# Cosine attention and a low-rank mixer on one core: transposing q and k by the DMA queue instead of TensorE from the ninth head pair on

## The chip, the core and the metric

The kernel runs on one core of a Trainium2 chip. A core has five engines that run side by side: TensorE (PE in the profile; its weight loads are PEld), VectorE (DVE), ScalarE (ACT), GpSimd (POOL) and SyncE (SP, which here only issues DMAs). Sixteen DMA engines move data between the main memory (DRAM), and SBUF, the memory on chip; a DMA can also go from SBUF to SBUF. TensorE writes its results to PSUM. The metric is the device time of one execution in microseconds (us). Before the change it is 648.73 us, the median of 9 runs (648.23 to 649.25).

## The reference

For 8 batches, 12 heads, 448 positions and 64 channels per head:

```python
q_n = q / (np.linalg.norm(q, axis=-1, keepdims=True) + 1e-06)
k_n = k / (np.linalg.norm(k, axis=-1, keepdims=True) + 1e-06)
scores = np.matmul(q_n, k_n.transpose(0, 1, 3, 2)) / tau
attn = softmax(scores)            # written out in the reference
x = (attn @ v) heads side by side # (8, 448, 768)
u = x + (x.transpose(0, 2, 1) @ U @ V).transpose(0, 2, 1)   # U 448x32, V 32x448
out = u + np.maximum(u @ w_ch1, 0) @ w_ch2                  # 768 -> 3072 -> 768
```

The scores need q and k with the 64 channels along the partitions, so both are transposed after they have been normalised.

## The kernel before

**Pairs and slots.** Two heads are worked on together. There are 48 pairs, 6 for each batch. The main loop (from L507) goes over 49 slots; slot n issues, in this order, the parts: `step_S` of pair n, first half; `step_V` of pair n-1, first half; `step_S`, second half; `step_V`, second half; `step_T` of pair n+1; `step_A` and `step_H` of pair n-1.

- `step_T` (L254) transposes the normalised q and k of a pair on TensorE: eight 128x128 transposes (L260) into the PSUM tile `tp`, one VectorE copy (L262) into the SBUF tile `qkT`, of which there are three in turn.
- `step_S` (L268) reads `qkT`: seven matmuls for the scores (L282, L274) and their exponentials on ScalarE (L284, L276).
- `step_V` (L290) multiplies with the values (L302, L309), and VectorE divides by the sums (L315, L316) into `X`.
- `step_A` and `step_H` (L327, L345) apply the low-rank mixer and add x; their result is u of the batch.

**Filling work.** Each batch's two large matrix products (`steps_m1`, L363, and `steps_m2`, L390 and L399) are cut into steps of about 1 us, put in a list when the batch's attention is finished, and handed out between the parts of the next batch's slots, in proportion to the parts' weights (`weights`, L520). The first such work is handed out in slot 7; what is left after the last slot runs at the end. ScalarE or VectorE takes each step's result out of PSUM, whichever a running estimate (`est`) finds free first.

**Loads and normalising.** q, k and v come in groups of mostly two pairs. Three sets of staging tiles (`qst`, `kst`, `vst`) are used in turn. A group's ten loads are issued on SP at the end of the slot before a group three earlier begins (L500, `load_all`). `Prep` normalises a group, m being its first pair: squares on GpSimd in slot m-3, sums, roots and reciprocals in slot m-2, and in the same slot the scaling (`scale`, L241), of k on GpSimd into `kb`, of q on VectorE into `qn`. The weight matrices are loaded on the GpSimd queue in slots 1 to 4.

**What sets the order.** Every engine's order is the order in which the program issues its instructions; nothing is rearranged. SP's queue holds, in that order, the loads of q, k and v and the stores of the output (L416, L419, L422), which wait until the `o_sb` tile is filled. An instruction that waits holds up all behind it on its engine. Eight semaphores are used in turn for SP's DMAs, so that each DMA waits for the eighth before it.

Of the kernel before, what the change touches and what calls it, by code (L numbers as in the profile page):

```python
# [10 lines left out]
BF = mybir.dt.bfloat16  # L11
# [11 lines left out]
def kernel(  # L23
# [16 lines left out]
    nc = tc.nc  # L40

    B, H, S, D = q.shape
# [3 lines left out]
    NP = H // 2  # L46
# [5 lines left out]
    const = ctx.enter_context(tc.tile_pool(name="const", bufs=1))  # L52
    work = ctx.enter_context(tc.tile_pool(name="work", bufs=2))
# [5 lines left out]
    class Estimate:  # L59


        def __init__(self):
            self.t = {"pe": 0.0, "act": 0.0, "dve": 0.0}
# [22 lines left out]

    NG = 4
    NST = 3
    qst, kst, vst, kbs, v65 = [], [], [], [], []
    for i in range(NST):  # L90
        for lst, nm in ((qst, "qst"), (kst, "kst"), (vst, "vst")):
            lst.append(const.tile([128, NG, 4, D], FP, name=f"{nm}{i}"))
        kbs.append(const.tile([128, NG // 2, 4, 2, D], BF, name=f"kb{i}"))
        v65.append(const.tile([128, NG, 4, D + 1], BF, name=f"v65_{i}"))
    for i in range(NST):
        nc.vector.memset(qst[i][64:128, :, 3, :], 0.0)
# [3 lines left out]
    ident = const.tile([128, 128], BF, name="ident")  # L100
# [7 lines left out]
    for i in range(2):  # L108
        t = const.tile([128, 7, 512], BF, name=f"E{i}")
# [75 lines left out]
    norm = {}  # L185

    class Prep:


        def __init__(self, gi):  # L190
            self.gi = gi
            _, _, self.n = groups[gi]
            self.nh = 2 * self.n
            self.s = gi % NST
            self.early = gi < 2
            self.ss = self.inv = self.qn = None
            self.sq = {}

        def flat(self, t):
# [34 lines left out]
            est.dve(0.55)  # L234

        def scale(self, i, j, eng):
            if self.qn is None:
                self.qn = work.tile([128, NG // 2, 4, 2, D], BF, name="qn", tag="qn", bufs=2)
            t, o = ((qst[self.s], self.qn), (kst[self.s], kbs[self.s]))[i]
            iv = self.inv[:, i, 8 * j:8 * j + 8].rearrange("p (h c) -> p c h", c=4)  # L240
            eng.tensor_mul(o[:, j, :, :, :],  # L241
                           t[:, 2 * j:2 * j + 2, :, :].rearrange("p h c d -> p c h d"),
                           iv.unsqueeze(3).to_broadcast([128, 4, 2, D]))
            if eng is nc.vector:
                est.dve(0.79)
            norm[self.gi] = (self.qn, kbs[self.s], v65[self.s])

        def values(self):
            nc.gpsimd.tensor_copy(out=self.flat(v65[self.s])[:, :, 0:D], in_=self.flat(vst[self.s]))
# [2 lines left out]
    qkT = {}  # L252

    def step_T(b, p):  # L254
        gi, j = group_of[(b, p)]
        qn, kb, _ = norm[gi]
        tp = psum.tile([128, 8, 128], BF, name="tp", tag="ps_x", bufs=1)
        for i, t in ((0, qn), (1, kb)):
            for c in range(4):
                nc.tensor.transpose(out=tp[:, 4 * i + c, :], in_=t[:, j, c, :, :], identity=ident)  # L260
        t = work.tile([128, 2, 512], BF, name="qkT", tag="qkT", bufs=3)
        nc.vector.tensor_copy(out=t.rearrange("p a b -> p (a b)"),  # L262
                              in_=tp.rearrange("p a b -> p (a b)"))
        qkT[(b, p)] = t
        est.pe(0.46)
        est.dve(0.69)

    def step_S(b, p, cs):  # L268
        t = qkT[(b, p)]
        e = E[(b * NP + p) % 2]  # L270
        for c in cs:
            sc = psum.tile([128, 2, 512], FP, name="sc", tag="ps_sc", bufs=2)
            if c == 3:
                nc.tensor.matmul(out=sc[:, 0, 0:S], lhsT=t[:, 1, 384:512], rhs=t[:, 0, 0:S],  # L274
                                 start=True, stop=True)
                nc.scalar.activation(out=e[:, 6, 0:S], in_=sc[:, 0, 0:S], func=AF.Exp)  # L276
                est.pe(0.3)
                est.act(0.56)
                continue
            for h in range(2):  # L280
                r = slice(64 * h, 64 * h + 64)
                nc.tensor.matmul(out=sc[:, h, 0:S], lhsT=t[r, 1, c * 128:(c + 1) * 128],  # L282
                                 rhs=t[r, 0, 0:S], start=True, stop=True)
            nc.scalar.activation(out=e[:, 2 * c:2 * c + 2, 0:S], in_=sc[:, :, 0:S], func=AF.Exp)  # L284
            est.pe(0.25)
            est.act(0.93)
# [2 lines left out]

    def step_V(b, p, half):  # L290
        gi, j = group_of[(b, p)]
        vv = norm[gi][2]
        e = E[(b * NP + p) % 2]
        if half == 0:
            X_of[(b, p)] = work.tile([128, 4, 128], BF, name="X", tag="X", bufs=2)
        X = X_of[(b, p)]
        bank = psum.tile([128, 512], FP, name="av", tag="ps_av", bufs=1)
        av_of[(b, p)] = bank
        av = bank[:, 0:4 * (D + 1)].rearrange("p (i h d) -> p i h d", i=2, h=2)
        for i in range(2):  # L300
            ic = 2 * half + i
            nc.tensor.matmul(out=av[:, i, :, :], lhsT=e[:, 6, ic * 128:(ic + 1) * 128],  # L302
                             rhs=vv[:, 2 * j:2 * j + 2, 3, :],
                             start=(i == 0), stop=False, skip_group_check=True)
        for i in range(2):
            ic = 2 * half + i
            for h in range(2):
                for c in range(3):
                    nc.tensor.matmul(out=av[:, i, h, :],  # L309
                                     lhsT=e[:, 2 * c + h, ic * 128:(ic + 1) * 128],  # L310
                                     rhs=vv[:, 2 * j + h, c, :],
                                     start=False, stop=(i == 1 and h == 1 and c == 2),
                                     skip_group_check=True)
        rd = work.tile([128, 4, 1], FP, name="rd", tag="rd", bufs=4)
        nc.vector.reciprocal(out=rd, in_=av.rearrange("p i h d -> p (i h) d")[:, :, D:D + 1])  # L315
        nc.vector.tensor_mul(  # L316
            X[:, 2 * half:2 * half + 2, :].rearrange("p i (h d) -> p i h d", h=2),
            av[:, :, :, 0:D],
            rd.rearrange("p (i h) o -> p i h o", h=2).to_broadcast([128, 2, 2, D]))
        est.pe(0.52)  # L320
        est.dve(0.6)
# [23 lines left out]
    def step_H(b, p):  # L345
        up = up_of[(b, p)]
        nc.tensor.matmul(out=up, lhsT=A_of[(b, p)], rhs=V_sb,  # L347
                         start=False, stop=True, skip_group_check=True)
        nc.vector.tensor_copy(out=u_of(b)[:, p, 0:S], in_=up)  # L349
        est.pe(0.19)  # L350
        est.dve(0.62)
        if b % 2 == 1 and p == NP - 1:
            nc.vector.tensor_copy(out=uO[:, :, S:512], in_=uE[:, :, 384:S])
# [77 lines left out]
    pairs = [(b, p) for b in range(B) for p in range(NP)]  # L431
# [36 lines left out]
    place_mixer()  # L468
    g1.reduce(1)
    step_T(*pairs[0])  # L470
    g1.reduce(0)
    g1.root()
# [9 lines left out]
    for gi in range(1, len(groups)):  # L482
        m, n, g = first_pair[gi], groups[gi][2], preps[gi]
# [23 lines left out]
    for n in range(NPAIR + 1):  # L507
        b, p = pairs[n] if n < NPAIR else (B, 0)
        prev = pairs[n - 1] if n > 0 else None
        now, nxt = n < NPAIR, n + 1 < NPAIR  # L510
        parts = [
            now and (lambda: step_S(b, p, (0, 1))),
            prev and (lambda: step_V(*prev, 0)),
            now and (lambda: step_S(b, p, (2, 3))),
            prev and (lambda: step_V(*prev, 1)),
            nxt and (lambda: step_T(*pairs[n + 1])),
            prev and (lambda: step_A(*prev)),
            prev and (lambda: step_H(*prev)),
        ]
        weights = [w if part else 0 for part, w in zip(parts, (2, 2, 2, 2, 2, 2, 1))]  # L520
        left = NP - p + 0.85 if p else 0.85
        nf = len(fill) if p == 0 else int(round(len(fill) / left))
        given = acc = 0
        for fn in after.pop((n, -1), []):
            fn()
        for i, (fn, w) in enumerate(zip(parts, weights)):
            if fn:
                fn()
            for g in after.pop((n, i), []):
                g()  # L530
            acc += w
            want = nf * acc // sum(weights)
            for _ in range(min(want - given, len(fill))):
                fill.pop(0)()
            given = want
        if p == 0 and n > 0:
            while fill:
                fill.pop(0)()
            fill.extend(steps_m1(b - 1) + steps_m2(b - 1))
# [38 lines left out]
```

## Time and profile before

| | |
|---|---|
| median of 9 runs | 648.73 us |
| the profiled execution: its own time, its span | 649.25 us, 647.5 us |
| TensorE busy | 609.6 us (94%) |
| VectorE, ScalarE, GpSimd busy | 273.3, 273.4, 195.1 us |
| L260, transposes on TensorE | 384, 219 ns each at the median |
| L262, VectorE's copy of a pair's transposes | 48, 687 ns in the mean |
| DMA traffic | 54.33 MB, mean 84 GB/s |

A line of the profile's groups names a source line, an engine, an operation, the tiles it writes and reads, its shapes and its count. Durations of TensorE's matmuls overlap one another, so that the time one takes up is read from the start of one to the start of the next in the timeline. In the timeline, a line is start, length, engine, line, operation, tiles, count, and in brackets idle time before it and what ended it. SPq is SP's queue: the time at which a DMA is issued, not the time that it takes. The table of DMA issues has the median time from issue to landing.

### The profile page before, as it was taken

What the parts mean: (1) busy time and instruction counts of PE and PEld (TensorE: products, weight loads), DVE (VectorE), ACT (ScalarE), POOL (GpSimd) and SP (SyncE); (2) the same over time, 40 slices, a digit from 0 to 9 for tenths busy, and PEclk for the clock granted to TensorE, in tenths of its full rate; (3) what the DMA queues carried; (4) which work ended last, traced back from release to release, by engine and by line L of the source; (5) the groups of instructions that cost most, each with busy time, mean ns of one, the idle gap of its engine ahead of it and who ended that gap; (6) DMA issues with size and microseconds to landing.
All of it is one profiled execution on the core that took longest, in us unless ns stands there. A gap on an engine that the chain in (4) does not pass through costs nothing.

```text
span 647.5 us, 12173 instructions
## 1 busy us (share of the span) xinstructions
PE 609.6 (94%) x5160; PEld 360.6 (56%) x5160; DVE 273.3 (42%) x524; ACT 273.4 (42%) x501; POOL 195.1 (30%) x158
## 2 busy tenths in 40 slices
PE   1467999999999999999999999999999999999997
PEld 0244556665566556665566655665566655665564
DVE  4688334355344454354352553463442543210000
ACT  2465554435433454344433455334523454424310
POOL 7877243042140341340431431431404401000000
PEclk9997999999999999999999999999999999999999
DMA  7799991350315420161315303044301100011012
GB/s 190 197 218 234 233 238 51 93 152 2 86 29 131 110 71 18 27 172 48 86 26 135 93 23 82 25 115 108 87 19 32 50 1 1 25 25 26 1 49 49
DMA packets 51782, 54.33 MB, mean 84 GB/s; under 512 B 5552, under 2 KB 48112, under 8 KB 51728
## 3 DMA queue, kind: packets, MB, share of 16 engines
q1 hardware_dynamic: 44288, 43.14, 25.9%
q0 software_dynamic: 7120, 10.18, 8.6%
q8 instruction: 40, 0.66, 0.4%
q10 hardware_dynamic: 320, 0.23, 0.1%
q14 instruction: 14, 0.11, 0.1%
HBM read 52.02 MB, written 11.01 MB: 97 GB/s over the span
## 4 chain that ended last, share of the span: by engine, by line
PE 91%; DVE 6%; DMA 2%; SPq 0%; issue 0%; ACT 0%; ACTq 0%
PE mp L390 34%; PE mp L363 34%; PE av L309 5%; PE sc L282 5%; PE tp L260 3%; PE sc L274 2%; DVE qn L241 2%; PE av L302 2%; PE av L331 2%; PE up L342 1%; PE mp L399 1%; DVE ss L215 1%; PE up L347 1%; DMA qst<-in_q_dram 1%; DVE qkT L262 1%; DVE X L316 1%
## 5 line engine op out<-in xcount | busy, mean ns | idle before, releaser
L390 PE MATMUL mp<-w_sb,relu 128*128 128x384 bf16 x1344 | 246.8, 326 | 0.0
L390 PEld LDWEIGHTS <-relu 128*128 128x128 bf16 x1344 | 123.7, 98 | 77.9 <-issue 7.4
L241 POOL TENSOR_TENSOR kb<-kst,inv 128x512 bf16<-128x512 f32 x46 | 59.3, 1309 | 336.5 <-DVE inv L233 301.1
L363 PEld LDWEIGHTS <-w_sb 128*128 128x128 bf16 x1152 | 106.1, 98 | 92.9 <-issue 7.8
L284 ACT ACTIVATE E<-sc 128x896 bf16<-128x896 f32 x144 | 126.1, 917 | 46.3 <-PE sc L282 46.2
L367 ACT ACTIVATE relu<-mp 128x448 bf16<-128x448 f32 x156 | 84.9, 544 | 134.3 <-PE mp L363 134.3
L363 PE MATMUL mp<-uE,w_sb 128*128 128x448 bf16 x576 | 122.9, 353 | 1.1 <-DVE uE L349 1.1
L363 PE MATMUL mp<-uO,w_sb 128*128 128x448 bf16 x576 | 118.0, 353 | 0.0
L404 ACT COPY o_sb<-mp 128x384 f32<-128x384 f32 x50 | 24.0, 479 | 108.9 <-PE mp L399 108.9
L215 DVE TENSOR_REDUCE ss<-sq 128x16 f32<-128x1024 f32 (+1 forms) x50 | 58.1, 1166 | 4.2 <-ACT sq L207 4.2
L315 DVE RECIPROCAL rd<-av 128x4 f32<-128x4 f32 x96 | 17.1, 178 | 95.6 <-PE av L309 95.6
L241 DVE TENSOR_TENSOR qn<-qst,inv 128x512 bf16<-128x512 f32 x48 | 53.4, 1150 | 0.0
L282 PE MATMUL sc<-qkT 64*128 64x448 bf16 x288 | 45.6, 368 | 8.1 <-DVE qkT L262 6.1
L309 PE MATMUL av<-v,E 128*128 128x65 bf16 x1152 | 53.0, 195 | 0.0
L210 POOL TENSOR_TENSOR sq<-kst 128x1024 f32<-128x1024 f32 x23 | 52.0, 2261 | 3.2 <-DMA qst<-in_q_dram 3.2
L369 DVE TENSOR_SCALAR relu<-mp 128x448 bf16<-128x448 f32 x36 | 22.5, 625 | 67.0 <-PE mp L363 67.0
L262 DVE COPY qkT<-tp 128x1024 bf16<-128x1024 bf16 x48 | 33.0, 687 | 36.6 <-PE tp L260 36.6
L309 PEld LDWEIGHTS <-E 128*128 128x128 bf16 x1152 | 46.3, 99 | 0.0
L210 POOL TENSOR_TENSOR sq<-qst 128x1024 f32<-128x1024 f32 x23 | 43.5, 1891 | 0.0
L316 DVE TENSOR_TENSOR X<-av,rd 128x256 bf16<-128x256 f32 x96 | 40.7, 424 | 3.3
L334 ACT CAST A_sb<-av 128x128 bf16<-128x128 f32 x48 | 12.7, 264 | 62.0 <-PE av L331 62.0
L349 DVE CAST uO<-up 128x448 bf16<-128x448 f32 x24 | 15.0, 623 | 53.9 <-PE up L347 53.9
(66 smaller groups left out, 394.6 us busy)
## 6 DMA issues: line engine op xcount, KB each, us to landing
out_dram<-o_sb SPq DMA_DIRECT2D x54, 192.0 KB, 2.7
w_sb<-in_moe_w_ch_dram POOLq DMA_DIRECT2D x8, 1152.0 KB, 26.6
qst<-in_q_dram SPq DMA_DIRECT2D x23, 256.0 KB, 3.8
vst<-in_v_dram SPq DMA_DIRECT2D x46, 128.0 KB, 2.9
kst<-in_k_dram SPq DMA_DIRECT2D x44, 128.0 KB, 3.6
qst<-in_q_dram SPq DMA_DIRECT2D x23, 192.0 KB, 4.0
vst<-in_v_dram SPq DMA_DIRECT2D x46, 96.0 KB, 2.6
kst<-in_k_dram SPq DMA_DIRECT2D x44, 96.0 KB, 3.4
```

The lines of the kernel that those rows point to most:

```text
L210: nc.gpsimd.tensor_mul(sq[:, 0:self.nh * 4, :], self.flat(t), self.flat(t))
L215: nc.vector.reduce_sum(self.ss[:, j, 0:self.nh * 4], self.sq[j][:, 0:self.nh * 4, :], axis=AX.X)
L241: eng.tensor_mul(o[:, j, :, :, :], t[:, 2 * j:2 * j + 2, :, :].rearrange("p h c d -> p c h d"), iv.unsqueeze(3).to_broadcast([128, 4, 2, D]))
L262: nc.vector.tensor_copy(out=t.rearrange("p a b -> p (a b)"), in_=tp.rearrange("p a b -> p (a b)"))
L282: nc.tensor.matmul(out=sc[:, h, 0:S], lhsT=t[r, 1, c * 128:(c + 1) * 128], rhs=t[r, 0, 0:S], start=True, stop=True)
L284: nc.scalar.activation(out=e[:, 2 * c:2 * c + 2, 0:S], in_=sc[:, :, 0:S], func=AF.Exp)
L309: nc.tensor.matmul(out=av[:, i, h, :], lhsT=e[:, 2 * c + h, ic * 128:(ic + 1) * 128], rhs=vv[:, 2 * j + h, c, :], start=False, stop=(i == ...
L316: nc.vector.tensor_mul(X[:, 2 * half:2 * half + 2, :].rearrange("p i (h d) -> p i h d", h=2), av[:, :, :, 0:D], rd.rearrange("p (i h) o -> ...
L363: nc.tensor.matmul(out=mp, lhsT=w1_sb[:, cc, f * 128:(f + 1) * 128], rhs=u[:, cc, 0:S], start=(cc == 0), stop=(cc == CC - 1))
L367: nc.scalar.activation(out=relu[:, f, o:o + S], in_=mp, func=AF.Relu)
L390: nc.tensor.matmul(out=mp, lhsT=relu[:, f, r0:r0 + 128], rhs=w2_sb[:, f, half * HC:(half + 1) * HC], start=(f == 0), stop=False, skip_grou ...
L404: nc.scalar.copy(out=o[:, cols], in_=mp)
```

## The change

From pair 8 on (`NP + 2`, NP being 6), `step_T` issues one transposing DMA on SP's queue, from SBUF to SBUF, in place of the eight TensorE transposes and the copy. So that one DMA can read q and k of a pair in one row per partition, both are scaled into one tile `qks` (three in turn, one for each set of staging tiles) instead of `qn` and `kbs`. For these pairs `step_T` is called at the start of slot n, ahead of all its parts, and no longer as the fifth part; that part's weight then is 0. The first eight pairs are transposed on TensorE as before.

```diff
-        kbs.append(const.tile([128, NG // 2, 4, 2, D], BF, name=f"kb{i}"))
+        qks.append(const.tile([128, NG // 2, 2, 4, 2, D], BF, name=f"qk{i}"))
...
         def scale(self, i, j, eng):
-            if self.qn is None:
-                self.qn = work.tile([128, NG // 2, 4, 2, D], BF, name="qn", tag="qn", bufs=2)
-            t, o = ((qst[self.s], self.qn), (kst[self.s], kbs[self.s]))[i]
+            t = (qst, kst)[i][self.s]
             iv = self.inv[:, i, 8 * j:8 * j + 8].rearrange("p (h c) -> p c h", c=4)
-            eng.tensor_mul(o[:, j, :, :, :],
+            eng.tensor_mul(qks[self.s][:, j, i, :, :, :],
...
     def step_T(b, p):
         gi, j = group_of[(b, p)]
-        qn, kb, _ = norm[gi]
+        qk, _ = norm[gi]
+        t = work.tile([128, 2, 512], BF, name="qkT", tag="qkT", bufs=3)
+        qkT[(b, p)] = t
+        if b * NP + p >= NP + 2:
+            nc.sync.dma_start_transpose(out=t.rearrange("p a (c r) -> p (a c) r", r=128),
+                                        in_=qk[:, j, :, :, :, :].rearrange("p i c h d -> p (i c h d)"))
+            return
         tp = psum.tile([128, 8, 128], BF, name="tp", tag="ps_x", bufs=1)
-        for i, t in ((0, qn), (1, kb)):
+        for i in range(2):
             for c in range(4):
-                nc.tensor.transpose(out=tp[:, 4 * i + c, :], in_=t[:, j, c, :, :], identity=ident)
-        t = work.tile([128, 2, 512], BF, name="qkT", tag="qkT", bufs=3)
+                nc.tensor.transpose(out=tp[:, 4 * i + c, :], in_=qk[:, j, i, c, :, :], identity=ident)
         nc.vector.tensor_copy(out=t.rearrange("p a b -> p (a b)"),
                               in_=tp.rearrange("p a b -> p (a b)"))
-        qkT[(b, p)] = t
...
-            nxt and (lambda: step_T(*pairs[n + 1])),
+            nxt and n + 1 < NP + 2 and (lambda: step_T(*pairs[n + 1])),
...
         for fn in after.pop((n, -1), []):
             fn()
+        if nxt and n + 1 >= NP + 2:
+            step_T(*pairs[n + 1])
         for i, (fn, w) in enumerate(zip(parts, weights)):
```

More of the change, by code (lines that the diff above doesn't have):

```diff
@@ L88 @@
     NST = 3
-    qst, kst, vst, kbs, v65 = [], [], [], [], []
+    qst, kst, vst, qks, v65 = [], [], [], [], []
     for i in range(NST):
@@ L195, in __init__ @@
             self.early = gi < 2
-            self.ss = self.inv = self.qn = None
+            self.ss = self.inv = None
             self.sq = {}
@@ L245, in scale @@
                 est.dve(0.79)
-            norm[self.gi] = (self.qn, kbs[self.s], v65[self.s])
+            norm[self.gi] = (qks[self.s], v65[self.s])
         def values(self):
@@ L291, in step_V @@
         gi, j = group_of[(b, p)]
-        vv = norm[gi][2]
+        vv = norm[gi][1]
         e = E[(b * NP + p) % 2]
```

## The prediction

> **What bounds the kernel now.** I read the page's summary first, then the table by stage, then the timelines of TensorE and of the SP queue, because the change moves work from the one to the other. From the page, in order: the span, TensorE's busy share, the DMA engines over 40 slices, and the chain that ended last by engine.
>
> ```profile
> span 647.5 us, 12173 instructions
> PE 609.6 (94%) x5160; PEld 360.6 (56%) x5160; DVE 273.3 (42%) x524; ACT 273.4 (42%) x501; POOL 195.1 (30%) x158
> DMA  7799991350315420161315303044301100011012
> PE 91%; DVE 6%; DMA 2%; SPq 0%; issue 0%; ACT 0%; ACTq 0%
> ```
>
> TensorE is the chain. The table by stage (stretch, its length, busy time of PE, PEld, DVE, ACT, POOL, granted clock, DMA share, GB/s) says where:
>
> ```profile
> 0.00:66.00 66.00, 32.59 (x360) 20.18 (x361) 47.57 (x95) 30.69 (x54) 50.74 (x64) 0.95 0.96 210
> 66.00:103.00 37.00, 37.00 (x305) 20.49 (x302) 13.81 (x27) 21.60 (x41) 10.92 (x8) 1.00 1.04 220
> 200.00:300.00 100.00, 100.00 (x859) 58.73 (x857) 47.60 (x88) 44.37 (x82) 30.83 (x20) 1.00 0.31 80
> ```
>
> Up to 66 us TensorE is half idle. From 66 us on it never waits: every wait of TensorE in the table of waits lies before. So each TensorE instruction removed after 66 us shortens the run, and each microsecond that TensorE is made to wait lengthens it. The DMA engines are saturated until about 97 us (share 1.04) because the two weight matrices stream in beside the loads, and nearly idle later.
>
> **The change part by part.**
>
> *Removed from TensorE.* 40 pairs (8 to 47) lose 8 transposes each, in slots 7 to 46, which all lie after 62.5 us. A slot in the timeline of TensorE:
>
> ```profile
> 291.55 2.43 PE L363 MATMUL mp<-uO,w_sb 128*128 128x448 bf16 x12
> 293.82 0.39 PE L260 MATMUL tp<-ident,qn 128*128 128x128 bf16 x4
> 294.04 0.39 PE L260 MATMUL tp<-ident,kb 128*128 128x128 bf16 x4
> 294.27 1.30 PE L363 MATMUL mp<-uO,w_sb 128*128 128x448 bf16 x6
> ```
>
> The instruction's own duration (219 ns) overlaps its neighbours. What counts is from the first transpose's start to the next matmul's, 294.27 - 293.82 = 0.45 us; two other slots (70.37 to 70.82, 307.26 to 307.71) give the same. 40 x 0.45 = **-18.0 us**.
>
> *Removed from VectorE.* 40 copies of 0.69 us, 27.5 us. VectorE is 42% busy and TensorE waits for it nowhere after 66 us: 0. The six waits of L342 for this copy (3.0 us in total) lie before 66 us, where the transposes stay.
>
> *Scaling into one tile.* The same instructions with the same elements (1309 ns on GpSimd, 1150 ns on VectorE), other addresses: 0.
>
> *Weights of the slot's parts.* A part that is not there has weight 0, so the filling matmuls are shared out over 11 instead of 13, and the step that sat between V's second half and A is gone. By the order of the changed kernel 6 filling matmuls at the least stay between them (0.97 us for L390, 1.14 us for L363). X is ready 0.85 us after V (V ends at 306.13, L316 at 306.98). One L369 of 0.62 us ahead of it on VectorE would make TensorE wait 0.5. Bounds 0 and 40 x 0.1 = 4; I take **+0.5**, since the nearest row (0.85 against 0.97) has no wait.
>
> *The transposes on the SP queue.* Each moves 256 KB, SBUF to SBUF: 10.5 MB beside 54.33 MB. What decides is when each lands against the S step (L282) of its pair. SP issues strictly in the program's order, and each DMA waits until the eighth before it has landed. So I laid the 40 transposes between the SP issues of the trace, by the changed kernel's order, and compared the end of the issue before with the start of S of the pair. Most have 9 to 46 us. Two places have not.
>
> First place, pairs 8 and 9. Pair 8's transpose comes right behind the last load at 68.21 and takes the place of the load at 69.48 (the issue lines, and the table of DMA issues of 68 to 69 us with its time to landing; then S of pair 8):
>
> ```profile
> 68.21 0.60 SPq L183 DMA_DIRECT2D vst<-in_v_dram  x1
> 69.48 0.59 SPq L175 DMA_DIRECT2D qst<-in_q_dram  x1
> vst<-in_v_dram SPq DMA_DIRECT2D x1, 128.0 KB, 11.1
> ...
> 76.07 0.55 PE L282 MATMUL sc<-qkT 64*128 64x448 bf16 x4
> ```
>
> The load at 68.21 landed at 79.3, the 256 KB load behind it at 69.48 + 12.6 = 82.1: seven DMAs lay ahead, and one load's turn comes every 1.4 us (2.8 us for 256 KB). A transpose in that place lands at 82.1 by bytes. If it counts by packets of 256 B, 1024 of them at the 128 per 1.4 us of the loads take 11.2 us, 90.5. S wants it at 76.07 - 0.45 = 75.6: a wait of **6.5**, up to 14.9. SP has the rest of load 8 between pair 8's and pair 9's transpose, and three of its issues wait for the transpose and what follows: by that pace pair 9's is issued at 89 with 9.8 us of loads ahead, less as the weights end at 97: it lands at about 98.5. S of pair 9 (88.37 before) would start at 82.1 + 12.3 - 0.45 = 94.0, so **4.5** more: 11.0 together. By the upper end S of pair 9 would start at 102.4 and its data come at 104.6: 17.1 together. The lower end is 0, if a transpose is not held behind the loads; no load in this stretch landed under 11 us before 86 us, so I take **+11.0**.
>
> After such a wait TensorE starts slowly. The nearest rows: after 5.35 us of idleness the four matmuls of S took 0.93 instead of 0.55 us, and the stretch from 26.50 to 30.05 took 3.55 us for about 2.0 us of work; after 1.06 us (65.20) nothing slowed.
>
> ```profile
> 26.50 0.93 PE L282 MATMUL sc<-qkT 64*128 64x448 bf16 x4 [5.35 <-DVE qkT L262]
> 32.02 0.55 PE L282 MATMUL sc<-qkT 64*128 64x448 bf16 x4
> ```
>
> The first wait's ramp disappears in the second wait; the second (4.5 less 1.5 = 3.0 us) lies between the two rows: 0 to 1.5, **+1.0**.
>
> The Trainium skill, "TensorE: Matmul & The Clock Gate", rules for kernels, asks for no gaps over about 3 us between bursts, or the clock halves; by it this term would be the full 1.5; the granted clock printed for the slow stretch is 1.00.
>
> Second place, pairs 13, 25 and 37. In slot 11 (23, 35) a store blocks SP until 124.3, the ten loads of a group follow, and pair 13's transpose comes only behind them:
>
> ```profile
> 124.34 0.60 SPq L419 DMA_DIRECT2D out_dram<-o_sb  x1
> 125.04 0.65 SPq L175 DMA_DIRECT2D qst<-in_q_dram  x1
> ...
> 131.03 0.60 SPq L183 DMA_DIRECT2D vst<-in_v_dram  x1
> ...
> 134.78 0.55 PE L282 MATMUL sc<-qkT 64*128 64x448 bf16 x4
> ```
>
> It can go at 131.6, S wants it at 134.78, less 0.45: 2.7 us (281.8 to 284.9 and 431.9 to 435.1 give the same). The last load lands 2.7 us after its issue, at 133.7. The transpose behind it: at 219 GB/s, the rate of this stretch, 1.2 us more, 3.3 from its issue; by packets (25.9% of 16 engines' span over 44288 packets is 61 ns each) 1024 x 61 ns / 16 = 3.9 us more, 6.0 from its issue. No row shows a transpose; the middle is 4.7, a wait of 2.0. Three of them: **+6.0**, bounds 1.8 and 9.9. The next smallest margins are 9.2 us (pairs 19, 31, 43) and 10 us (12, 20, 24, 32, 36, 44): they hide a landing time under 9 us at no cost.
>
> Sum: -18.0 + 0.5 + 11.0 + 1.0 + 6.0 = **+0.5 us** on the profiled execution's own 649.25 (span 647.5 and 1.75 around it), 649.75; the median of the runs is 0.52 lower, so **649.2**.
>
> The Trainium skill, "VectorE: DVE Perf Modes", the three transpose paths, speaks against the change: it gives 1309 ns for a 128x128 transpose by DMA against 390 ns on TensorE. Eight in a row would be an estimated 10.5 us, the margins of 2.7, 9.2 and 10 us would all be passed, and the sum would be near +23, 672. "Advanced Engine Details and Errata", X-bar transpose, says that such DMAs run about as fast as ordinary ones; by that the landing is the 3.3 us and the sum -3.7, 645. No run so far shows either.
>
> **The rivals.** *Packets (slower).* A transpose is dear because it goes in small pieces: 17.1 for the first place, 9.9 for the second, 1.5 ramp: -18.0 + 0.5 + 17.1 + 1.5 + 9.9 = +11, 660. For it: with the weights, loads of 96 KB and 128 KB (128 packets each) took the same 1.4 us, so the queue goes by packets. Against: nothing says that a transpose's packets are that small. It decides from a landing time of 4.5 us on.
>
> *Nothing is late (faster).* The transposes do not wait behind the loads and land in 3 us: -18.0 + 0.5 + 1 = 632. For it: after 100 us the DMA engines are under a third busy. Against: the 11 to 14 us of all loads between 60 and 86 us. It needs pair 8's data within 6.1 us of 69.5; with the first place at half price, it gives 640.
>
> *The DMA queue becomes the bound (slower).* If one transpose takes 12 us, margins of 9 to 10 us fail too, three to four times in each 150 us: three times 9.3 + 2.0 + 2.8 = 42 on top of -18 + 11 + 1, 685. Against: 256 KB loads land in 3.7 us.
>
> **How the numbers follow.** About 0.2% (1.3 us) is what a measurement can tell from no change: 647.4 to 650.0. The forecast's own case, 644 to 651, has 0.45: 0.17 of it under 647.4, 0.18 within, 0.10 over. Packets, 651 to 664: 0.28. Nothing late, 630 to 644: 0.15. The queue as the bound, over 664: 0.12. Faster 0.15 + 0.17 = 0.32, same 0.18, slower 0.10 + 0.28 + 0.12 = 0.50. The range leaves out the last case and half of the fast one: 638 to 664.
>
> **What would show it.** L260 with 64 instead of 384 matmuls; two waits of PE L282 for a DMA at 76 to 99 us, 11 us together, and three of about 2 us, at pairs 13, 25 and 37; the transposes' issues on SP with a landing time of 4 to 5 us in quiet stretches and 12 us at the first. Wrong it is if the first lands much earlier or later than 82, if waits appear at pairs other than these five, or if A waits for X.

## The result, and the profile after

The changed kernel takes 650.86 us (median of 10 runs, 649.39 to 652.65; the record lists an eleventh, 653.19, which this median leaves out) against 648.62 us for the kernel before (31 runs): a ratio of 1.0034, 95% interval 1.0027 to 1.0042. It is slower by 0.34%, which is clear of no change; the forecast of 649.2 us was 1.7 us low and its range held the result.

The profiled execution of the changed kernel is the fastest of its runs, 649.39 us, with a span of 647.6 us against 647.5 us before. So the profile shows how some 18 us were gained and lost again, and not the last 1.5 us by which the median lies above it. From its page, the same lines as before, with the packets and with the group of TensorE's S step:

```profile
span 647.6 us, 11611 instructions
PE 593.6 (92%) x4840; PEld 343.3 (53%) x4840; DVE 243.1 (38%) x481; ACT 275.1 (42%) x504; POOL 195.8 (30%) x158
DMA packets 94021, 64.79 MB, mean 100 GB/s; under 512 B 47792, under 2 KB 90352, under 8 KB 93968
PE 85%; DMA 10%; DVE 2%; SPq 2%; issue 0%; ACT 0%
L284 PE MATMUL sc<-qkT 64*128 64x448 bf16 x288 | 46.0, 371 | 25.0 <-DMA qkT<-qk 16.9
```

TensorE is 16 us less busy and the span is the same: DMA is now 10% of the chain (2% before), 5% of it the transposes and 4% loads of k. The last line says how long TensorE stood still for it: 16.9 us of waiting of the S step for a transposing DMA. The packets under 512 B rose from 5552 to 47792, 42240 more, which is 1056 for each of the 40 transposes: they move in pieces of 256 B (1024 of them are the 256 KB).

The table by stage (columns as before) puts the loss before 110 us:

```profile
66.00:110.00 44.00, 31.13 (x234) 16.29 (x233) 9.42 (x20) 18.43 (x35) 10.29 (x7) 0.84 1.05 204
87.93:91.01 3.08, 3.08 (x11) 1.02 (x11) 0.00 (x0) 1.73 (x2) 0.00 (x0) 0.50 1.14 233
110.00:200.00 90.00, 88.97 (x729) 51.31 (x728) 37.67 (x72) 39.12 (x73) 28.02 (x19) 1.00 0.38 85
300.00:400.00 100.00, 100.00 (x819) 57.12 (x817) 40.96 (x80) 46.57 (x86) 30.84 (x20) 1.00 0.45 98
```

The timeline of SP, the DMA issue with its time to landing, and the timeline of TensorE at that place:

```profile
67.49 0.60 SPq L183 DMA_DIRECT2D vst<-in_v_dram  x1
68.85 6.01 SPq L258 DMA_TRANSPOSE qkT<-qk  x1
74.97 0.62 SPq L175 DMA_DIRECT2D qst<-in_q_dram  x1
...
qkT<-qk SPq DMA_TRANSPOSE x1, 19.0
...
73.77 1.30 PE L365 MATMUL mp<-uE,w_sb 128*128 128x448 bf16 x6
87.93 0.93 PE L284 MATMUL sc<-qkT 64*128 64x448 bf16 x4 [12.87 <-DMA qkT<-qk]
88.79 2.39 PE L365 MATMUL mp<-uE,w_sb 128*128 128x448 bf16 x6
91.01 0.29 PE L304 MATMUL av<-v,E 128*128 128x130 bf16 x2
```

Pair 8's transpose is issued at 68.85, lands 19.0 us later, and S of pair 8, whose turn came at 75.1, starts at 87.9. Then the clock is slow: from 87.93 to 91.01 the granted clock was 0.50, and TensorE did in 3.08 us what had taken 1.63 us before (76.07 to 77.70), 1.45 us more. The packets of that stretch, from the first 256 B piece of the transpose to its last (a line is a queue with its packets, MB and share of the 16 engines; q0 is the weights' queue, q1 is SP's):

```profile
q0 software_dynamic: 1119, 1.67, 93.8%
q1 hardware_dynamic: 1119, 0.32, 24.0%
```

So the 19.0 us are 8.3 us until the first piece, at 77.2, while the loads ahead of it were moved, and then 10.1 us in which SP's packets and the weights' went one for one. Pair 9 brings no second wait: its transpose landed 5.0 us after its issue at 94.58, S came at 101.25.

The other waits after 66 us are three, at pairs 13, 25 and 37, each behind the ten loads of a group:

```profile
146.95 0.55 PE L284 MATMUL sc<-qkT 64*128 64x448 bf16 x4 [1.03 <-DMA qkT<-qk]
292.52 0.55 PE L284 MATMUL sc<-qkT 64*128 64x448 bf16 x4 [0.70 <-DMA qkT<-qk]
439.70 0.55 PE L284 MATMUL sc<-qkT 64*128 64x448 bf16 x4 [2.31 <-DMA qkT<-qk]
```

Together 12.87 + 1.45 + 4.04 = 18.4 us lost. In quiet stretches a transpose is quick: 3.4 us to landing in the median, and SP is held 1.27 us by each.

### The profile page after: what moved, and what is told of

Same layout as the page of the kernel before. It is cut to its first block, busy times and chain, and to the rows that moved or that the text cites. A ratio compares the mean times of both kernels' runs of the same rounds, so it can differ in the third digit from the quotient of the medians.

```text
span 647.6 us, 11611 instructions
## 1 busy us (share of the span) xinstructions
PE 593.6 (92%) x4840; PEld 343.3 (53%) x4840; DVE 243.1 (38%) x481; ACT 275.1 (42%) x504; POOL 195.8 (30%) x158
## 2 busy tenths in 40 slices
DMA packets 94021, 64.79 MB, mean 100 GB/s; under 512 B 47792, under 2 KB 90352, under 8 KB 93968
## 4 chain that ended last, share of the span: by engine, by line
PE 85%; DMA 10%; DVE 2%; SPq 2%; issue 0%; ACT 0%
PE mp L392 33%; PE mp L365 33%; PE sc L284 5%; PE av L311 5%; DMA qkT<-qk 5%; DMA kst<-in_k_dram 4%; PE sc L276 2%; PE av L304 2%; PE av L333 1%; PE mp L401 1%; PE up L344 1%; PE up L349 1%; DMA qst<-in_q_dram 1%; DVE qk L239 1%; DVE ss L215 1%; SPq L175 0%
## 5 line engine op out<-in xcount | busy, mean ns | idle before, releaser
L392 PE MATMUL mp<-w_sb,relu 128*128 128x384 bf16 x1344 | 243.2, 326 | 0.0
L239 POOL TENSOR_TENSOR qk<-kst,inv 128x512 bf16<-128x512 f32 x46 | 68.0, 1498 | 339.6 <-DVE inv L233 325.4
L365 PE MATMUL mp<-uO,w_sb 128*128 128x448 bf16 x576 | 116.5, 353 | 0.0
L406 ACT COPY o_sb<-mp 128x384 f32<-128x384 f32 x53 | 25.4, 479 | 115.8 <-PE mp L401 114.9
L284 PE MATMUL sc<-qkT 64*128 64x448 bf16 x288 | 46.0, 371 | 25.0 <-DMA qkT<-qk 16.9
L239 DVE TENSOR_TENSOR qk<-qst,inv 128x512 bf16<-128x512 f32 x48 | 53.0, 1143 | 0.7
L210 POOL TENSOR_TENSOR sq<-kst 128x1024 f32<-128x1024 f32 x23 | 44.0, 1912 | 2.5 <-DMA qst<-in_q_dram 2.5
L284 PEld LDWEIGHTS <-qkT 64*128 64x128 bf16 x288 | 10.7, 94 | 52.6 <-issue 26.2
L351 DVE CAST uE<-up 128x448 bf16<-128x448 f32 x24 | 15.0, 623 | 50.2 <-PE up L349 50.2
```

The costliest lines, as they stand in the source:

```text
L210: nc.gpsimd.tensor_mul(sq[:, 0:self.nh * 4, :], self.flat(t), self.flat(t))
L239: eng.tensor_mul(qks[self.s][:, j, i, :, :, :], t[:, 2 * j:2 * j + 2, :, :].rearrange("p h c d -> p c h d"), iv.unsqueeze(3).to_broadcast( ...
L365: nc.tensor.matmul(out=mp, lhsT=w1_sb[:, cc, f * 128:(f + 1) * 128], rhs=u[:, cc, 0:S], start=(cc == 0), stop=(cc == CC - 1))
L392: nc.tensor.matmul(out=mp, lhsT=relu[:, f, r0:r0 + 128], rhs=w2_sb[:, f, half * HC:(half + 1) * HC], start=(f == 0), stop=False, skip_grou ...
L406: nc.scalar.copy(out=o[:, cols], in_=mp)
```

## The experiments

The theory was that two places of lateness eat the whole gain, each with a cause of its own: the weights' traffic at pair 8, and ten loads ahead on SP's queue at pairs 13, 25 and 37. The rivals: the first transposing DMA is slow because it is the first; the weights' traffic alone does it, whatever lies ahead; it is the transposing that is slow, not the small pieces.

**e1: begin at pair 10.**

```diff
-        if b * NP + p >= NP + 2:
+        if b * NP + p >= 10:
...
-            nxt and n + 1 < NP + 2 and (lambda: step_T(*pairs[n + 1])),
+            nxt and n + 1 < 10 and (lambda: step_T(*pairs[n + 1])),
...
-        if nxt and n + 1 >= NP + 2:
+        if nxt and n + 1 >= 10:
```

> The changed kernel, but with pairs 8 and 9 still transposed on TensorE (the DMA path begins at pair 10). Theory (queue): the first transpose was late because it lay behind seven loads in SP's queue while the weights streamed in, and because its small packets took turns with the weights' packets. Then pair 10's transpose, issued at about 86 us, lands at 96 to 98 us, before its S step at about 99.8, and no wait over 3 us is left after 66 us: 38 x 0.45 = 17.1 us gained, 4.0 lost again at the three late pairs, about 636 us. Rival (first use): the first transposing DMA is slow in itself, 19 us from issue to landing wherever it stands: it lands at 105, a wait of 5 us and a slow start of 1.5, about 642 us.

```profile
86.50 5.67 SPq L258 DMA_TRANSPOSE qkT<-qk  x1
qkT<-qk SPq DMA_TRANSPOSE x1, 10.9
100.39 0.55 PE L284 MATMUL sc<-qkT 64*128 64x448 bf16 x4
```

Measured: 635.95 us against 648.99 us before on the same chip, ratio 0.980 (0.9785 to 0.9815). The first transpose was issued at 86.50 and landed 10.9 us later, at 97.4, ahead of its S step at 100.39. Its pieces moved from 94.4 us on, and the weights' last packet came at 95.8. No early wait is left, and the three late ones add up to 4.0 us as before. The first of all transposes is thus not slow for being the first.

**e2: a quarter of the weight traffic.** Every matmul of the two products uses the first six blocks of 128, so that their results are not the reference's.

```diff
-    put(1, 4, lambda: (load_w1(0, 768), load_w1(768, 1536)))
-    put(2, 4, lambda: (load_w1(1536, 2304), load_w1(2304, 3072)))
-    put(3, 4, lambda: (load_w2(0, 6), load_w2(6, 12)))
-    put(4, 4, lambda: (load_w2(12, 18), load_w2(18, 24)))
+    put(1, 4, lambda: load_w1(0, 768))
+    put(3, 4, lambda: load_w2(0, 6))
...
-                nc.tensor.matmul(out=mp, lhsT=w1_sb[:, cc, f * 128:(f + 1) * 128],
+                nc.tensor.matmul(out=mp, lhsT=w1_sb[:, cc, (f % 6) * 128:(f % 6 + 1) * 128],
...
-                                 rhs=w2_sb[:, f, half * HC:(half + 1) * HC],
+                                 rhs=w2_sb[:, f % 6, half * HC:(half + 1) * HC],
```

> The changed kernel with a quarter of the weight traffic: only the first 768 columns of the first matrix and the first 6 of 24 row blocks of the second are loaded, and every matmul uses those (so the products are not the reference's; the count of matmuls is the same). Queue theory: SP is not backed up, pair 8's transpose goes as soon as its tile is scaled, at about 64.6 us, and lands in 3 to 5 us; no wait at pair 8; span 14.5 us shorter than the changed kernel's, about 633 us. First use: 19 us to landing again, at 83.6, a wait of 8 us, span about 642.

Measured: span 632.0 us, one run. Pair 8's transpose was issued at 62.02 and landed 3.1 us later; no wait at pair 8; three waits of 3.5 us in all remain at the late pairs. While it ran, from 63.3 to 64.7 us, SP's queue was the only one that moved packets:

```profile
62.02 1.68 SPq L258 DMA_TRANSPOSE qkT<-qk  x1
q1 hardware_dynamic: 1056, 0.26, 101.8%
```

Its 1024 pieces went in 1.4 us, against 10.1 us beside the weights: small pieces are not slow by themselves. With fewer weights the loads ahead had landed too, so this run takes away both; e3 parts them.

**e3: transposes ahead of the loads, from pair 8 on.**

```diff
-            put(m - 1, 6, lambda gi=gi: load_all(gi + 3))
+            put(*((7, 0) if gi == 4 else (m - 1, 6)), lambda gi=gi: load_all(gi + 3))
...
-        if nxt and n + 1 >= NP + 2:
+        if nxt and n + 1 >= 8 and n % 2 == 1:
             step_T(*pairs[n + 1])
+            step_T(*pairs[n + 2])
```

> The changed kernel with both transposes of a group issued together, at the start of the slot before its first pair, and the fifth group's ten loads put behind pair 8's and 9's transposes. So no load lies ahead of a transpose for long, while the weights still stream in. Queue theory: pair 8's transpose is issued at about 65 us and only takes turns with the weights, landing after 8 to 9 us at 73 to 74, before 75.1; no wait at pairs 8 and 9, nor at pairs 13, 25 and 37: 18 us gained, about 631 us. Rival (weights alone): the weights' traffic by itself makes a transpose take 19 us, whatever is ahead in the queue: it lands at 84, a wait of 9 us and 1.5 of slow start, about 641 us. First use: the same 641.

Measured: 635.63 us, ratio 0.980 (0.9783 to 0.9821), 4.6 us above the expectation. The waits at pairs 13, 25 and 37 are gone, as expected. But pair 8's transpose, issued at 62.86 with no load less than 12 us old ahead of it, still took 14.0 us:

```profile
62.86 1.36 SPq L258 DMA_TRANSPOSE qkT<-qk  x1
...
qkT<-qk SPq DMA_TRANSPOSE x1, 14.0
...
76.86 0.55 PE L284 MATMUL sc<-qkT 64*128 64x448 bf16 x4 [1.63 <-DMA qkT<-qk]
102.70 0.55 PE L284 MATMUL sc<-qkT 64*128 64x448 bf16 x4 [2.06 <-DMA qkT<-qk]
```

S waited 1.63 us at pair 8, and 2.06 us at pair 10, whose transpose came to stand behind the loads that had been pushed back. My 8 to 9 us for taking turns with the weights alone was too little, and the rival's 19 too much. The packets say where the 14.0 us went. From 62.86 to 66.7 us nothing of SP's queue moved, only the weights did; from 66.7 on the 1024 pieces took 9.2 us, again one for one with the weights:

```profile
q0 software_dynamic: 521, 0.80, 114.6%
...
q0 software_dynamic: 1064, 1.59, 94.4%
q1 hardware_dynamic: 1050, 0.26, 21.7%
```

So of the 19.0 us in the changed kernel some 4 go to the loads ahead (8.3 us to the first piece, against 3.9 here) and 9 to 10 to the turns beside the weights. Why the first piece comes only after 3.9 us here, and after 1.3 us in e2, is not shown.

**e4: ScalarE's queue.**

```diff
-            nc.sync.dma_start_transpose(out=t.rearrange("p a (c r) -> p (a c) r", r=128),
+            nc.scalar.dma_start_transpose(out=t.rearrange("p a (c r) -> p (a c) r", r=128),
```

> The changed kernel with the transposes issued on ScalarE's queue in place of SP's. Queue theory: nothing lies ahead of them in a queue of their own, so pair 8's lands within 9 us of its issue at 64.6 and the three late pairs are never late; but ScalarE is held by each issue (1.27 us at the median on SP, 6.0 at the first), waits for the scaling at the start of slot 7, and its exponentials come later: TensorE then waits 0 to 0.5 us in a slot and up to 6 us in slot 7. Span 633 to 645. Weights alone: 19 us to landing for pair 8 all the same, a wait of about 8 us, span 642 to 655.

Measured: span 642.8 us, one run, within the expected 633 to 645 and within the rival's 642 to 655 too, so that the span decides nothing. ScalarE issued pair 8's transpose at 69.96, 9 us after its instruction before; its queue held back the exponentials, and TensorE waited 5.73 us for them. The transpose landed 16.3 us after its issue with nothing ahead in its own queue, and TensorE waited 3.35 us more. Its first piece moved at 74.1, and from then to 85.5 three queues ran, the weights', SP's and ScalarE's (q10):

```profile
q0 software_dynamic: 1044, 1.58, 75.5%
q1 hardware_dynamic: 1044, 0.86, 29.2%
q10 hardware_dynamic: 1033, 0.26, 10.7%
```

Each had a third of the packets. So not even a queue of its own makes it quick beside the weights. The late waits are gone. Until 69.96 ScalarE did not wait for the scaled tile, which VectorE and GpSimd had finished by 64.1. The eighth load before the transpose in SP's queue was issued at 56.23 and landed 13.6 us later, at 69.8; that fits a DMA on ScalarE's queue waiting for its turn of the eight semaphores as one on SP's does.

**e5: both remedies, from pair 10 on and ahead of the loads.**

```diff
-        if b * NP + p >= NP + 2:
+        if b * NP + p >= 10:
...
-        if nxt and n + 1 >= NP + 2:
+        if nxt and n + 1 >= 10 and n % 2 == 1:
             step_T(*pairs[n + 1])
+            step_T(*pairs[n + 2])
```

> Both remedies at once: the DMA path begins at pair 10, and both transposes of a group are issued together, ahead of the next group's loads. Theory: each place of lateness has its own cause (the weights' traffic at the first; ten loads ahead in SP's queue at pairs 13, 25 and 37), so both waits go: no wait of TensorE for a transpose after 66 us, 38 x 0.45 = 17.1 us gained and nothing given back, about 632 us. Rival: two transposes back to back hold each other and the loads up, so that waits of 1 to 2 us appear at other pairs, 634 to 637 us.

Measured: 632.22 us (631.94 to 632.51) against 648.77 us, ratio 0.9742 (0.9729 to 0.9755). After 66 us TensorE waits for nothing at all. The gain is 16.55 us between the medians. In the profiled executions S of pair 9 starts 0.21 us earlier than before (88.16 against 88.37) and S of pair 47 17.19 us earlier (545.33 against 562.52): 16.98 us for 38 pairs, 0.447 us for a pair. The lines are of the kernel before, then of e5:

```profile
88.37 0.55 PE L282 MATMUL sc<-qkT 64*128 64x448 bf16 x4
562.52 0.55 PE L282 MATMUL sc<-qkT 64*128 64x448 bf16 x4
...
88.16 0.55 PE L284 MATMUL sc<-qkT 64*128 64x448 bf16 x4
545.33 0.55 PE L284 MATMUL sc<-qkT 64*128 64x448 bf16 x4
```

The end behind pair 47 is 0.47 us longer, with TensorE no busier. This is the fastest of the kernels whose output is the reference's, and 2.6% faster than the kernel before. The rival's waits at other pairs did not come.

**e6, e7, e8: what is slow beside the weights?** All 48 pairs are transposed on TensorE, and one more DMA of the same 256 KB goes into a spare tile at pair 8's place in SP's queue; nothing waits for it. Only the form of this DMA differs.

```diff
...
-        if nxt and n + 1 >= NP + 2:
-            step_T(*pairs[n + 1])
+        if n + 1 == NP + 2:
+            qk8 = norm[group_of[pairs[n + 1]][0]][0]
+            nc.sync.dma_start_transpose(out=spare[:, :, 0:128],                       # e6
+                in_=qk8[:, 0, :, :, :, :].rearrange("p i c h d -> p (i c h d)"))
+            nc.sync.dma_start(out=spare.rearrange("p a b -> p (a b)")[:, 0:1024],     # e7
+                in_=qk8[:, 0, :, :, :, :].rearrange("p i c h d -> p (i c h d)"))
+            nc.sync.dma_start(out=spare[:, :, 0:128],                                 # e8
+                in_=qk8[:, 0, :, :, :, :].rearrange("p i c h d -> p (i c) (h d)"))
```

> All 48 pairs transposed on TensorE, and one transposing DMA of pair 8's scaled tile into a spare tile, at the place in SP's queue where the changed kernel has pair 8's; nothing waits for it. Measures its landing without a stall of TensorE around it. By packets: 1056 packets that each wait a turn, landing 17 to 21 us after its issue at about 69; by bytes (256 KB like a load of q): 13 us. Span as before, 646 to 649 us.

> The same place and the same 256 KB as a plain copy, SBUF to SBUF, in 128 rows of 2 KB. By packets: 128 turns, so it lands 12 to 13 us after its issue, like a load of 128 packets. By bytes: 13 us. If whatever goes from SBUF to SBUF beside the weights were slow: 17 us and more. Span as before, 646 to 649 us.

> The same copy in 1024 pieces of 256 B, no transposing. By packets: 1024 turns, landing 17 to 21 us after its issue, like the transposing DMA. Rival (the transposing is what is slow): 12 to 13 us, like the copy in 2 KB rows. Span as before, 646 to 649 us.

Measured, one run each, times 648.4 to 648.7 us. The tables of DMA issues around 69 us, of e6, e7 and e8 in this order:

```profile
spare<-qk SPq DMA_TRANSPOSE x1, 19.6
```

```profile
spare<-qk SPq DMA_DIRECT2D x1, 256.0 KB, 11.6
```

```profile
spare<-qk SPq DMA_DIRECT2D x1, 256.0 KB, 18.9
```

The plain copy in pieces of 256 B is as slow as the transposing DMA, 18.9 against 19.6 us; the same bytes in rows of 2 KB land after 11.6 us, as soon as a load. In all three the first 8.3 or 8.4 us go by behind the loads ahead; then the 128 rows take 2.8 us, the 1024 pieces 10.1 us as a copy and 10.7 us as a transpose. So it is the pieces, not the transposing. The queues of e6 from 69 to 82 us show why:

```profile
q0 software_dynamic: 1336, 2.00, 86.4%
q1 hardware_dynamic: 1332, 0.84, 29.4%
```

The weights' queue (q0) and SP's (q1) had the same number of packets, with very different bytes. While both have packets waiting, a queue gets as many through as the other, whatever their size: a transpose asks for 1056 such turns, a copy in 2 KB rows for 128 or so.

## Why the prediction was right, and where it was off

Its sum against the runs, in us:

| term | predicted | measured |
|---|---|---|
| transposes off TensorE | -18.0 | -17.9 (40 x 0.447, from e5) |
| wait at pairs 8 and 9 | +11.0 (6.5 + 4.5) | +12.87 (12.87 + 0) |
| slow clock after it | +1.0 | +1.45 |
| waits at pairs 13, 25, 37 | +6.0 | +4.04 |
| A waiting for X | +0.5 | 0 |
| sum | +0.5 | +0.46 |

The profiled span went up by 0.14 (647.46 to 647.60). The stretch before pair 7's S took 0.62 us less in this execution (S starts at 61.92 against 62.54), and 0.3 us are assigned to nothing. That the sums agree so well is in part luck: the wait at pair 8 was 6.4 us longer than predicted, and the one at pair 9, the late pairs and A's wait together 7.0 us shorter.

*What bounds the kernel, and what is removed.* Right: TensorE's time after 66 us counted fully, at 0.447 us a pair against the 0.45 read from the timeline. VectorE's 27.5 us less were worth nothing, as said: TensorE waits for VectorE nowhere after 66 us, before or after. A did not wait for X either, so that the +0.5 was not needed; no run parts the 6 matmuls of cover from VectorE's freed time. Only the durations were not the same: GpSimd's scaling took 1498 instead of 1309 ns, its squares of k 1912 instead of 2261. In e6, with the same tile `qks`, they took 1311 and 2262, so it is not the addresses; after 66 us TensorE waited for neither.

*First place.* The mechanism was right: pair 8's transpose behind the loads, beside the weights. The mis-sized term is its landing. I took 82.1 by bytes; it came at 87.9, near the 90.5 that I had kept as the upper end by packets, and well after the 82 by which the prediction wanted to be judged; e6 to e8 show that packets decide. The row that should have told me stood in the text: loads of 96 and 128 KB, with 128 packets each, took the same 1.4 us. The second step, 4.5 us at pair 9, failed with it: since the first wait was longer, S of pair 9 came later (101.25 against 94.0) and found its data, landed at 99.6. The two errors nearly cancel, by luck. So with the slow clock: it was counted behind a second wait of 3.0 us that did not come, and it followed the first; the size, 1.45, is the upper end of the 0 to 1.5.

*Second place.* The right three pairs, and no other. The transposes landed 3.3, 3.3 and 4.9 us after their issue (predicted 4.7), so the three waits were 1.03, 0.70 and 2.31 instead of 2.0 each. In quiet stretches the lower end, 3.3 by bytes, was right at two of the three; at the third the 256 B pieces had all moved by 3.0 us too, and what held its landing until 4.9 is not shown.

*The rivals.* Packets: right at the first place, where another queue takes turns, and wrong at the second, where none does; its 660 us did not come. Nothing late: fell by the first wait. The queue as the bound: fell by the landing time of 3.4 us.

*What stays open.* The median lies 1.5 us above the profiled run, and the runs spread over 3.3 us (649.39 to 652.65), where e5's five spread over 0.6. That the waits for transposes vary from run to run would fit, but no trace of a slower run was looked at. And what passes between the issue of a transpose and its first piece beside the weights, 3.9 us in e3 and 4.1 in e4 against 1.3 in e2, is not shown.

## What to carry to other kernels

Before work is moved from the bounding engine to a DMA queue, lay its issues between those of the queue in the trace and read each one's margin against its first reader; the waits came at four of the five pairs that this named, and at no other. Beside a second busy queue, count a DMA's packets and not its bytes: 256 KB took 11.6 us in 2 KB rows and 19 us in 256 B pieces. A change that comes out even may hold a gain: starting at pair 10, when the weights were at their end, and issuing ahead of the loads turned +0.3% into -2.6%.

## What the runs showed of the hardware that was not expected

- The transposing DMA held SP for 6.0 us beside the weights (1.27 us in quiet), and later issues for up to 3.75 us; the plain copy in 256 B pieces returned after 0.64 us, but the load behind it was held 4.62 us.
- The Trainium skill, "Advanced Engine Details and Errata", X-bar transpose, calls such DMAs as fast as ordinary ones. In quiet stretches that agrees (3.4 us, against 3.8 for a 256 KB load). Beside the weights it agrees with a copy in the same pieces of 256 B (19.6 against 18.9 us), and not with a copy of the same bytes in 2 KB rows (11.6).
- The Trainium skill, "VectorE: DVE Perf Modes", the three transpose paths, gives 1309 ns for one 128x128 transpose by DMA; eight of them in one DMA landed in 3.4 us, so that figure does not multiply.
